# A gated mix of a state-space layer and a two-layer network: the state product of the last two chunks as seven block products, with its skip term scaled by ScalarE and added by DMA

## The chip, the cores and the metric

The kernel runs on one core of one Trainium2 chip. The metric is device microseconds of one execution. A core has TensorE (PE, with its weight loads PEld), VectorE (DVE), ScalarE (ACT), GpSimd (POOL) and SyncE (SP), which run side by side, each through its own list of instructions in order, and wait for each other by semaphores. SP, ACT and POOL can start transfers (DMA).

## The reference, cut to what matters

The input x has 2048 rows of 640 columns. A gate per row mixes a diagonal complex state-space layer with a dense network.

```python
g = sigmoid((x * gate_w).sum(-1, keepdims=True))
# state layer
Bu = einsum("bld,pd->blp", x, B_bar)              # 640 complex states
for t in range(L):
    h = Lam_bar * h + Bu[:, t, :]                 # one step per row
y = 2.0 * einsum("blp,dp->bld", hseq, C).real + x * Dskip
# dense layer
b = gelu(x @ w1 + b1) @ w2 + b2                   # 640 -> 1728 -> 640
return g * y + (1 - g) * b
```

So the state product is hs (2048 x 1280: real and imaginary parts) times CT (1280 x 640), and x * Dskip is its skip term.

## The kernel before, in words

The 2048 rows go in four chunks of 512, each of four row tiles of 128. For each chunk there are four stages of TensorE work:

- `ssm(c)`: x times B, 50 matmuls of 512 columns. ScalarE copies each result out of PSUM (L610). VectorE then runs, for each of five state tiles, a rotation (f1 to f3: wa, wb, v at L533), two scans along time (L555) and a rotation back (f6 to f8: wa, wb, hs at L533).
- `ff1(c)`: x times w1 in 13 tiles and a narrow last one, each through a gelu on ScalarE (L308).
- `fin_b(c)`: the dense second product, already as seven block products. The hidden matrix of a chunk is cut into two row halves and two inner halves (a, b; s1, d), w2 into two inner and two column halves. Sums and differences of these blocks (N2, N3, TA, TB, TC) are made by ScalarE negations (`minus`, L655) followed by accumulating transfers (`plus`, L650) from the POOL queue. PSUM results are copied between banks by ScalarE (`fork`, L714), and what leaves is scaled by 1 - g into a tile `gb` (`out_of`, L722). Product Q is scaled into `gq` (`part_7`, L735) and added by one transfer per row tile to both halves of `gb`.
- `fin_a(c)`: the state product, plain: for each row tile and column half ten matmuls of 320 columns (L775). Before them ScalarE has copied the skip term x * Dskip, which VectorE made (`skip`, L635), into the PSUM bank (`seed`, L641), and the matmuls add to it. VectorE scales the sum by g, adds `gb` (L780) and SP stores the row tile (L790).

The order is written out by hand at the end of the program. VectorE's work is put into a list by `later` with a due time and a cost; `let_out` and `dve_now` let it out in that order as a hand-kept clock of TensorE moves on. So every engine has a fixed order, and `at` hooks place small steps between the products. From chunk 3 on it reads:

```python
    ssm(3)
    gel_tile(3)
    ff1(3)
    gates(3)
    skips(2)
    fin_b(2, seeds(2, lambda: minus_c(3)))
    minus_d(3)
    fin_a(2)
    skips(3)
    fin_b(3, seeds(3))
    let_out(1e9)
    fin_a(3)
```

PSUM has eight banks, and a bank is handed on when its last reader is done. Rows of x for the skip term are loaded into five rotating tiles `xn`.

Of the kernel before, what the change touches and what calls it, by code (L numbers as in the profile page):

```python
# [16 lines left out]
P = 128  # L17
# [25 lines left out]
def kernel(  # L43
# [41 lines left out]
    xT = [xA, xB, xB, xA]  # L85
    w1a = [const.tile([P, cut1], BF16, name=f"w1a_{kd}") for kd in range(KD)]
    w1b = [const.tile([P, cut2 - cut1], BF16, name=f"w1b_{kd}") for kd in range(KD)]
    w1c_lo = const.tile([P, 3, n1c], BF16, name="w1c_lo")
    w1c_hi = const.tile([P, 2, n1c], BF16, name="w1c_hi")
# [39 lines left out]
    def load_w1a(queue, kd):  # L129
        queue.dma_start(out=w1a[kd][:], in_=B_w1[kd * P:(kd + 1) * P, 0:cut1])  # L130

# [394 lines left out]
    def scan_ops(c, ks, bu, ready):  # L526
# [5 lines left out]
        def tt(o, a, b, op):  # L532
            nc.vector.tensor_tensor(out=o, in0=a, in1=b, op=op)  # L533
# [115 lines left out]
    def plus(dst, src):  # L649
        nc.gpsimd.dma_start(out=dst, in_=src, accum_op=ALU.add)  # L650
# [39 lines left out]

    def fin_b(c, at={}):
        (a, b), (s1, d) = blocks(c)
# [38 lines left out]
        def part_7():  # L731
            for j in range(H):
# [26 lines left out]
        settle()  # L759

    def fin_a(c, at={}):
        let_out(0, c)
        for a in range(TPC):
            ti = c * TPC + a
            lo = a * P
            ot = fwork.tile([P, D], BF16, name="ot", bufs=3)
            if a < TPC - 2:
# [3 lines left out]
            for i, (d0, d1) in enumerate(cuts(ti)):  # L771
                p = seeded[ti][i]
                for j in range(2 * KS):
                    CT = CT_re if j < KS else CT_im
                    nc.tensor.matmul(p[:, 0:d1 - d0], lhsT=hs[c][:, j, lo:lo + P], rhs=CT[:, j % KS, d0:d1],  # L775
                                     start=False, stop=(j == 2 * KS - 1), skip_group_check=True)
                    pe(d1 - d0)
# [86 lines left out]
```

## Time and profile before

| | |
|---|---|
| median of 3 runs | 211.99 us (211.9 to 212.34) |
| the profiled execution | 212.2 us, span of its instructions 210.4 us |
| granted TensorE clock | 1.00 throughout |
| VectorE, L555 scans that carry a state, 30 | 37.2 us, 1.271 each |
| VectorE, L780 outputs, 33 | 17.5 us, 0.531 each |
| ScalarE, L308 gelu, 52 | 32.9 us, 0.694 each |
| state product of chunk 0, 80 matmuls | 10.87 us |
| dense product of a chunk, 98 matmuls | some 13.3 us |

The page gives each engine's busy time and its share of the span; groups of equal instructions with count, mean duration and the idle time just before them; DMA queues with packets, bytes and the share of 16 engines' time; and the chain of work that ended last, followed back from the last instruction. The busy time of a pipelined engine overlaps at the edges, so two neighbours of 0.54 us can follow each other every 0.46 us.

### The profile page before, as it was taken

The numbers are of one execution on the slowest core, as the hardware profiler recorded it, in microseconds if no ns is written. First come the engines' busy times: TensorE is split into PE (matmuls) and PEld (weight loads), VectorE is DVE, ScalarE is ACT, GpSimd is POOL, SyncE is SP. The second block draws the span as 40 slices with busy tenths as digits, with TensorE's granted clock in tenths as the row PEclk, the third lists the DMA queues.
The fourth block names the chain that finished last, engine by engine and source line by source line (L and its number), as shares of the span: only waits on it lengthen the run. The fifth ranks groups of instructions, "written<-read, shape, count | busy, mean of one in ns | idle before, by whom it ended". The sixth has DMA issues, their size and how long they took to land.

```text
span 210.4 us, 3617 instructions
## 1 busy us (share of the span) xinstructions
PE 204.3 (97%) x1326; PEld 122.0 (58%) x1326; DVE 180.0 (86%) x295; ACT 142.7 (68%) x290; POOL 48.3 (23%) x79
## 2 busy tenths in 40 slices
PE   8999999989999998999999999999999999999994
PEld 5745444444477543576457777544447777767773
DVE  2579999999997899596999999999999999998132
ACT  3499979996768799990674896267586594047600
POOL 8345059314310500031001043200000145010400
PEclk9999999999999999999999999999999999999999
DMA  7999999999997250249842379910001629943721
GB/s 181 243 189 203 199 247 283 205 231 173 158 190 184 38 90 0 62 86 236 189 101 44 78 119 205 234 49 0 0 0 27 125 64 178 215 131 79 112 78 62
DMA packets 42582, 27.82 MB, mean 132 GB/s; under 512 B 26594, under 2 KB 40388, under 8 KB 42564
## 3 DMA queue, kind: packets, MB, share of 16 engines
q1 hardware_dynamic: 36628, 16.21, 32.4%
q0 software_dynamic: 5360, 10.89, 30.2%
q10 hardware_dynamic: 576, 0.49, 0.7%
q8 instruction: 10, 0.16, 0.3%
q14 instruction: 8, 0.07, 0.1%
HBM read 7.79 MB, written 2.62 MB: 49 GB/s over the span
## 4 chain that ended last, share of the span: by engine, by line
PE 45%; DVE 33%; ACT 12%; issue 5%; DMA 3%; SPq 1%; DVEq 0%
PE bank L607 15%; DVE g L555 11%; PE bank L702 10%; PE bank L775 10%; PE bank L299 8%; DVE wa L533 6%; DVE wb L533 6%; ACT gel L308 5%; DVE hs L533 3%; DVE v L533 3%; DMA xn<-in_A_x_dram 3%; DVE ot L780 3%; PE bank L323 1%; DVE xn L635 1%; ACT TB L655 1%
## 5 line engine op out<-in xcount | busy, mean ns | idle before, releaser
L775 PEld LDWEIGHTS <-hs 128*128 128x128 bf16 x330 | 31.6, 98 | 11.9
L555 DVE TENSOR_TENSOR_SCAN g<-r_c,carry,v 128x512 bf16<-128x512 f32 x30 | 37.2, 1271 | 0.8
L610 ACT ACTIVATE bu<-bank 128x512 bf16<-128x512 f32 x40 | 23.1, 594 | 19.0 <-PE bank L607 18.9
L308 ACT ACTIVATE gel<-bank,colB 128x512 bf16<-128x512 f32 (+1 forms) x52 | 32.9, 694 | 3.0 <-PE bank L299 2.8
L702 PEld LDWEIGHTS <-gel 128*128 128x128 bf16 x280 | 27.2, 98 | 11.0
L780 DVE SCALAR_TENSOR_TENSOR ot<-bank,gcol,gb 128x320 bf16<-128x320 f32 (+2 forms) x33 | 17.5, 531 | 11.8 <-PE bank L775 5.1
L775 PE MATMUL bank<-CT_im,hs 128*128 128x320 bf16 (+2 forms) x165 | 27.1, 295 | 0.0
L775 PE MATMUL bank<-CT_re,hs 128*128 128x320 bf16 (+2 forms) x165 | 27.1, 295 | 0.0
L702 PE MATMUL bank<-w_sb,gel 128*128 128x320 bf16 x168 | 24.1, 299 | 0.0
L299 PEld LDWEIGHTS <-w1a 128*128 128x128 bf16 x162 | 14.4, 101 | 11.9
L722 ACT ACTIVATE gb<-bank,gcol 128x320 f32<-128x320 f32 x32 | 16.1, 525 | 6.0 <-PE bank L702 6.0
L714 ACT ACTIVATE bank<-bank 128x320 f32<-128x320 f32 x16 | 6.8, 424 | 16.5 <-PE bank L702 16.5
L650 POOL DMA_DIRECT2D gel<-N x4 | 3.4, 856 | 60.8 <-PE bank L702 51.2
L607 PEld LDWEIGHTS <-BT_im 128*128 128x128 bf16 x100 | 9.8, 98 | 11.8
L607 PEld LDWEIGHTS <-BT_re 128*128 128x128 bf16 x100 | 9.6, 98 | 11.0
L650 POOL DMA_DIRECT2D gb<-gq x8 | 10.4, 1624 | 22.6 <-ACT gb L722 22.6
L533 DVE TENSOR_TENSOR v<-wa,wb 128x1024 bf16<-128x1024 bf16 (+1 forms) x25 | 14.2, 584 | 0.6
L299 PE MATMUL bank<-xA,w1a 128*128 128x128 bf16 (+2 forms) x102 | 14.6, 302 | 0.0
L533 DVE TENSOR_TENSOR wa<-TCOS,bu 128x1024 bf16<-128x1024 bf16 x20 | 13.7, 687 | 0.6
L533 DVE TENSOR_TENSOR wa<-TCOS,g 128x1024 bf16<-128x1024 bf16 x20 | 13.8, 688 | 0.4
L641 ACT ACTIVATE bank<-xn 128x320 f32<-128x320 bf16 (+2 forms) x33 | 12.7, 427 | 1.7 <-DVE xn L635 1.5
L533 DVE TENSOR_TENSOR wb<-TSIN,g 128x1024 bf16<-128x1024 bf16 x20 | 13.7, 683 | 0.0
(146 smaller groups left out, 354.7 us busy)
## 6 DMA issues: line engine op xcount, KB each, us to landing
gb<-gq POOLq DMA_DIRECT2D x8, 320.0 KB, 5.4
out_dram<-ot SPq DMA_DIRECT2D x15, 160.0 KB, 3.8
w_sb<-in_B_w_dram SPq DMA_DIRECT2D x4, 480.0 KB, 6.5
xn<-in_A_x_dram SPq DMA_DIRECT2D x12, 160.0 KB, 3.9
gel<-N POOLq DMA_DIRECT2D x4, 448.0 KB, 4.5
N<-gel POOLq DMA_DIRECT2D x3, 448.0 KB, 4.5
gel<-gel POOLq DMA_DIRECT2D x3, 448.0 KB, 6.4
N<-N POOLq DMA_DIRECT2D x3, 448.0 KB, 7.8
```

The costliest lines, as they stand in the source:

```text
L299: nc.tensor.matmul(p[:, t0:t1], lhsT=w, rhs=xT[c][:, kd, t0:t1], start=(kd == 0) if first is None else first, stop=(kd == last), skip_grou ...
L308: nc.scalar.activation(out=dst, in_=src, func=ACT.Gelu_apprx_tanh, bias=b1_c[p0:p1, kf:kf + 1])
L533: nc.vector.tensor_tensor(out=o, in0=a, in1=b, op=op)
L555: nc.vector.tensor_tensor_scan(s["g"][:, ri, :], r_c[:, ks:ks + 1].to_broadcast([P, CH]), s["v"][:, ri, :], init, ALU.mult, ALU.add)
L607: nc.tensor.matmul(p[:], lhsT=BT[ks >= KSA][:, kd, (ks % KSA if ks < KSA else ks - KSA) * P:][:, 0:P], rhs=xT[c][:, kd, :], start=(kd == 0 ...
L610: nc.scalar.activation(out=bu[:, ri, :], in_=p[:], func=ACT.Identity)
L641: nc.scalar.activation(out=p[:, 0:d1 - d0], in_=xn[ti][:, d0:d1], func=ACT.Identity)
L650: nc.gpsimd.dma_start(out=dst, in_=src, accum_op=ALU.add)
L702: nc.tensor.matmul(p[:, 0:HD], lhsT=lhs[:, s, j * P:(j + 1) * P], rhs=rhs[:, s, :], start=fresh and s == 0, stop=s == KH - 1, skip_group_c ...
L722: nc.scalar.activation(out=gbs[ti][:, h * HD:(h + 1) * HD], in_=quad[j][name][:, 0:HD], func=ACT.Identity, scale=gcol[:, 1, ti:ti + 1])
L775: nc.tensor.matmul(p[:, 0:d1 - d0], lhsT=hs[c][:, j, lo:lo + P], rhs=CT[:, j % KS, d0:d1], start=False, stop=(j == 2 * KS - 1), skip_group ...
L780: nc.vector.scalar_tensor_tensor(out=ot[:, d0:d1], in0=p[:, 0:d1 - d0], scalar=gcol[:, 0, ti:ti + 1], in1=gbs[ti][:, d0:d1], op0=ALU.mult, ...
```

## The change

For chunks 2 and 3, `fin_a` is replaced by `fin_s`, which makes the state product as seven block products of 256 x 640 by 640 x 320 instead of eight. hs is laid out by row half first, so that its four blocks a, b, g21, d lie in one piece each. CT's four blocks are turned once, during ff1(3), into the needed sums: two ScalarE negations (`c_minus`) and four accumulating transfers (`c_sums`), with one plain copy of a block ahead of them. The sums of hs (M2, M3, M4, and g21 + d in place) are made for chunk 2 by two negations, four accumulating transfers and one copy (`h_hooks`, in hooks of fin_b(2)); for chunk 3 by four VectorE operations (`h_sums`). They lie in tiles that are no longer needed.

The skip term no longer goes through PSUM: ScalarE scales x * Dskip by g into `GS` tiles (`gated`), and transfers add these to `gb` (`skip_in`, and for the lower row tiles together with `gq`). For these two chunks all four skip products of a chunk (`skips`) come ahead of fin_b. `xn` has four rotating tiles instead of five; each next load now follows the scaling. The output tile `ot` has four buffers instead of three.

In the matmuls of `fin_s`, X starts as a times C11 and grows by three products; Y takes X's first state plus b times C21; `less` subtracts product Q (kept in `gq`) from X into Z and later into Q's bank; `out_of` is what L780 did.

```diff
-    xnp = ctx.enter_context(tc.tile_pool(name="xnp", bufs=5))
+    xnp = ctx.enter_context(tc.tile_pool(name="xnp", bufs=4))
...
+            dst = hs[c][:].rearrange("p i r k t -> p r i k t")[:, :, :, ks, :]
             if signed:
-                return tt(hs[c][:].rearrange("p (r k) t -> p r k t", r=2)[:, :, ks, :], s["no"][:], s["ns"][:, ::-1, :], ALU.subtract)
+                return tt(dst, to(s["no"][:]), to(s["ns"][:, ::-1, :]), ALU.subtract)
...
-        hs[c] = hsp.tile([P, 2 * KS, CH], BF16, name="hs")
+        hs[c] = hsp.tile([P, 2, 2, KS, HT], BF16, name="hs")
...
-        if ti + 5 < NT:
-            load_xn(ti + 5)
+        if ti + TPC < NT:
+            load_xn(ti + TPC)
...
+    def twice(dst, src):
+        plus(dst.rearrange("p (h d) -> p h d", h=2), src[:].rearrange("p (o d) -> p o d", o=1).to_broadcast([P, 2, HD]))
...
         part_7()
+        for j in range(H if gs else 0):
+            twice(gs[H + j], gq[j])
+        hook(5)
         both("X", s1, TA)
...
         for j in range(H):
-            plus(gbs[c * TPC + H + j][:].rearrange("p (h d) -> p h d", h=2),
-                 gq[j][:].rearrange("p (o d) -> p o d", o=1).to_broadcast([P, 2, HD]))
+            if gs:
+                plus(gbs[c * TPC + H + j][:], gs[H + j])
+            else:
+                twice(gbs[c * TPC + H + j][:], gq[j])
...
+    def c_minus(h):
+        minus((UA, UB)[h], (C11, C22)[h], 1.6)
+
+    def c_sums():
+        for dst, src in ((UA, C12), (C12, UB), (UB, UA), (UC, UB)):
+            plus(dst, src)
...
+    def h_sums(c):
+        (a, b), (g21, d) = h_blocks(c)
+        for out, x, y, op in ((M3, a, g21, ALU.subtract), (g21, g21, d, ALU.add), (M2, a, g21, ALU.subtract), (M4, b, M2, ALU.add)):
+            dve_now(ck.dve, 0.85, lambda: nc.vector.tensor_tensor(out=flat(out), in0=flat(x), in1=flat(y), op=op))
+
+    def gated(c, a):
+        ti = c * TPC + a
+        nc.scalar.activation(out=GS[a], in_=xn[ti][:], func=ACT.Identity, scale=gcol[:, 0, ti:ti + 1])
+        act(0.82)
+        if ti + TPC < NT:
+            load_xn(ti + TPC)
+
+    def skip_in(c):
+        for j in range(H):
+            plus(gbs[c * TPC + j][:], GS[j])
+
+    def h_hooks(c):
+        (a, b), (g21, d) = h_blocks(c)
+        def first():
+            minus(M3, g21, 1.3)
+            plus(flat(M3), flat(a))
+        def second():
+            minus(M2, d, 1.3)
+            plus(flat(g21), flat(d))
+            nc.sync.dma_start(out=flat(M4), in_=flat(b))
+        return first, second, lambda: plus(flat(M2), flat(M3)), lambda: plus(flat(M4), flat(M2))
+
+    def fin_bs(c, h=[lambda: None] * 4):
+        fin_b(c, {0: h[0], 1: lambda: (h[1](), gated(c, H), gated(c, H + 1)), 5: h[2],
+                  2: lambda: gated(c, 0), 3: lambda: gated(c, 1), 4: lambda: (skip_in(c), h[3]())}, GS)
+
+    def fin_s(c, at={}):
...
+        for j in range(H):
+            product(X, j, a, C11, True)
+            product(Q, j, M3, C12, True)
+            Y[j] = bank()
+            nc.scalar.activation(out=Y[j][:, 0:HD], in_=X[j][:, 0:HD], func=ACT.Identity)
...
+            nc.scalar.activation(out=gq[j][:], in_=Q[j][:, 0:HD], func=ACT.Identity)
+            act(0.53)
+        hook(0)
+        for j in range(H):
+            product(X, j, M2, UB)
+            less(Z, j)
+        for j in range(H):
+            product(Y, j, b, C21)
+        hook(1)
+        for j in range(H):
+            product(X, j, s1, UA)
+            product(Z, j, d, UC)
+            less(Q, j)
+            out_of(Q, j, 1, 1)
+        for j in range(H):
+            out_of(Y, j, 0, 0)
...
+        for j in range(H):
+            out_of(Z, j, 1, 0)
+            store(j, 1)
...
+            product(X, j, M4, C22, False, cols)
+            for d0, d1 in cols:
+                out_of(X, j, 0, 1, d0, d1)
...
-    ff1(3)
+    nc.sync.dma_start(out=UC, in_=C21)
+    ff1(3, 0, {1: lambda: c_minus(0), 4: lambda: (c_minus(1), c_sums())})
     gates(3)
     skips(2)
-    fin_b(2, seeds(2, lambda: minus_c(3)))
-    minus_d(3)
-    fin_a(2)
+    skips(2, H)
+    let_out(0, 2)
+    fin_bs(2, h_hooks(2))
+    fin_s(2, {0: lambda: minus_c(3), 1: lambda: minus_d(3)})
     skips(3)
-    fin_b(3, seeds(3))
+    skips(3, H)
+    fin_bs(3)
     let_out(1e9)
-    fin_a(3)
+    h_sums(3)
+    fin_s(3)
```

In the prediction, the five matmuls of one block product and one row tile are called a product; a chunk's `fin_s` has fourteen of them, two for each of the seven.

More of the change, by code (lines that the diff above doesn't have):

```diff
@@ L85 @@
     xT = [xA, xB, xB, xA]
-    w1a = [const.tile([P, cut1], BF16, name=f"w1a_{kd}") for kd in range(KD)]
+    w1a_sb = const.tile([P, KD, cut1], BF16, name="w1a_sb")
+    w1a = [w1a_sb[:, kd, :] for kd in range(KD)]
     w1b = [const.tile([P, cut2 - cut1], BF16, name=f"w1b_{kd}") for kd in range(KD)]
-    w1c_lo = const.tile([P, 3, n1c], BF16, name="w1c_lo")
+    w1c_lo = const.tile([P, 3, n1c + 1], BF16, name="w1c_lo")
     w1c_hi = const.tile([P, 2, n1c], BF16, name="w1c_hi")
@@ L129, in load_w1a @@
     def load_w1a(queue, kd):
-        queue.dma_start(out=w1a[kd][:], in_=B_w1[kd * P:(kd + 1) * P, 0:cut1])
+        queue.dma_start(out=w1a[kd], in_=B_w1[kd * P:(kd + 1) * P, 0:cut1])
     def rows(queue, dst, v):
@@ L166 @@
     HC = CH // 8
-    tfi = work.tile([P, HC], I32, name="e")
+    tfi = work.tile([P, HC], I32, name="e", bufs=1)
     nc.gpsimd.iota(tfi[:], pattern=[[1, HC]], base=0, channel_multiplier=0)
@@ L213, in load_skip @@
             load_x0(nc.sync, a, KA * P, D)
-        load_xn(TPC)
     ctx.enter_context(tc.manual_schedule(engines={E.PE, E.DVE, E.Activation, E.SP, E.Pool}))
@@ L581, in f8 @@
         def f8():
+            to = lambda t: t.rearrange("p r (i t) -> p r i t", i=2)
+            dst = hs[c][:].rearrange("p i r k t -> p r i k t")[:, :, :, ks, :]
             if signed:
-                return tt(hs[c][:].rearrange("p (r k) t -> p r k t", r=2)[:, :, ks, :], s["no"][:], s["ns"][:, ::-1, :], ALU.subtract)
-            tt(hs[c][:, ks, :], s["no"][:, 0, :], s["ns"][:, 1, :], ALU.subtract)
-            tt(hs[c][:, KS + ks, :], s["ns"][:, 0, :], s["no"][:, 1, :], ALU.add)
+                return tt(dst, to(s["no"][:]), to(s["ns"][:, ::-1, :]), ALU.subtract)
+            for r, x, y, op in ((0, s["no"][:, 0:1, :], s["ns"][:, 1:2, :], ALU.subtract), (1, s["ns"][:, 0:1, :], s["no"][:, 1:2, :], ALU.add)):
+                tt(dst[:, r], to(x)[:, 0], to(y)[:, 0], op)
         later(ready, 0.68, f1)
@@ L689, in first_sums, with fin_b @@
         tt(N2[:], a, g21, ALU.subtract)
-    def fin_b(c, at={}):
+    def twice(dst, src):
+        plus(dst.rearrange("p (h d) -> p h d", h=2), src[:].rearrange("p (o d) -> p o d", o=1).to_broadcast([P, 2, HD]))
+    def fin_b(c, at={}, gs=None):
         (a, b), (s1, d) = blocks(c)
@@ L758, in fin_b @@
         out_of("X", 0, 1)
-        settle()
+        hook(4)
     def fin_a(c, at={}):
@@ L764, in fin_a @@
             ti = c * TPC + a
-            lo = a * P
-            ot = fwork.tile([P, D], BF16, name="ot", bufs=3)
+            ot = fwork.tile([P, D], BF16, name="ot", bufs=4)
             if a < TPC - 2:
@@ L774, in fin_a @@
                     CT = CT_re if j < KS else CT_im
-                    nc.tensor.matmul(p[:, 0:d1 - d0], lhsT=hs[c][:, j, lo:lo + P], rhs=CT[:, j % KS, d0:d1],
+                    nc.tensor.matmul(p[:, 0:d1 - d0], lhsT=hs[c][:, a // H, j // KS, j % KS, (a % H) * P:][:, 0:P], rhs=CT[:, j % KS, d0:d1],
                                      start=False, stop=(j == 2 * KS - 1), skip_group_check=True)
@@ L790, in fin_a @@
                 nc.sync.dma_start(out=out2d[ti * P:(ti + 1) * P, :], in_=ot[:])
-    def skips(c):
-        skip(c * TPC)
-        skip(c * TPC + 1)
+    narrow = lambda t, n: t.rearrange("p k t -> p (k t)")[:, 0:n]
+    UA, UB, UC = (narrow(t[:], KS * HD).rearrange("p (k d) -> p k d", k=KS) for t in (BT_re[1], BT_im[1], xB))
+    M2, M3 = (t[:].rearrange("p k t -> p (k t)").rearrange("p (k t) -> p k t", k=KS) for t in (BT_im[0], BT_re[0]))
+    M4 = narrow(xA[:], KS * HT).rearrange("p (k t) -> p k t", k=KS)
@@ new lines, with h_blocks @@
+    GS = [narrow(w1a_sb[:], 4 * D)[:, j * 2 * D:(j + 1) * 2 * D].bitcast(F32) for j in range(2)]
+    GS += [xA[:].rearrange("p k t -> p (k t)")[:, KS * HT:].bitcast(F32), narrow(w1c_lo[:], 2 * D).bitcast(F32)]
+    C11, C12, C21, C22 = (t[:, :, h * HD:(h + 1) * HD] for t in (CT_re, CT_im) for h in range(2))
+    def c_minus(h):
[3 more added lines that the diff above has]
+            plus(dst, src)
+    def h_blocks(c):
+        return [[hs[c][:, i, r] for r in range(2)] for i in range(2)]
@@ new lines, in fin_s, with product, less, out_of @@
+    def fin_s(c, at={}):
+        let_out(0, c)
+        (a, b), (s1, d) = h_blocks(c)
+        X, Y, Z, Q, gq = ([None] * H for _ in range(5))
+        ots = {}
+        def product(t, j, lhs, rhs, fresh=False, cols=((0, HD),)):
+            if fresh:
+                t[j] = bank()
+            for d0, d1 in cols:
+                for ks in range(KS):
+                    nc.tensor.matmul(t[j][:, d0:d1], lhsT=lhs[:, ks, j * P:(j + 1) * P], rhs=rhs[:, ks, d0:d1],
+                                     start=fresh and ks == 0, stop=ks == KS - 1, skip_group_check=True)
+                    pe(d1 - d0)
+            let_out(ck.pe)
+        def less(out, j):
+            t = out[j] = out[j] or bank()
+            dve_now(ck.pe + 0.2, 0.52, lambda: nc.vector.tensor_tensor(out=t[:, 0:HD], in0=X[j][:, 0:HD], in1=gq[j][:], op=ALU.subtract))
+        def out_of(t, j, half, h, d0=0, d1=HD, wait=0.2):
+            ti = c * TPC + half * H + j
+            if ti not in ots:
+                ots[ti] = fwork.tile([P, D], BF16, name="ot", bufs=4)
+            o = h * HD
+            dve_now(ck.pe + wait, 0.54, lambda: nc.vector.scalar_tensor_tensor(
+                out=ots[ti][:, o + d0:o + d1], in0=t[j][:, d0:d1], scalar=gcol[:, 0, ti:ti + 1],
+                in1=gbs[ti][:, o + d0:o + d1], op0=ALU.mult, op1=ALU.add))
+        def store(j, half, d0=0, d1=D, queue=None):
+            ti = c * TPC + half * H + j
+            (queue or nc.sync).dma_start(out=out2d[ti * P:(ti + 1) * P, d0:d1], in_=ots[ti][:, d0:d1])
+        def hook(i):
+            if i in at:
+                at[i]()
+            settle()
+        for j in range(H):
[3 more added lines that the diff above has]
+            nc.scalar.activation(out=Y[j][:, 0:HD], in_=X[j][:, 0:HD], func=ACT.Identity)
+            act(0.45)
+            gq[j] = fwork.tile([P, HD], F32, name="gq", bufs=2)
+            nc.scalar.activation(out=gq[j][:], in_=Q[j][:, 0:HD], func=ACT.Identity)
+            act(0.53)
+        hook(0)
+        for j in range(H):
[11 more added lines that the diff above has]
+            out_of(Y, j, 0, 0)
+        tail = c == NCH - 1
+        for j in range(H):
+            out_of(Z, j, 1, 0)
+            store(j, 1)
+            last = tail and j == H - 1
+            cols = ((0, 192), (192, HD)) if last else ((0, HD),)
+            product(X, j, M4, C22, False, cols)
+            for d0, d1 in cols:
+                out_of(X, j, 0, 1, d0, d1)
+            if not last:
+                store(j, 0)
+            else:
+                store(j, 0, 0, HD + 192)
+                store(j, 0, HD + 192, D, nc.scalar)
@@ L796, in seeds, with skips @@
+    def skips(c, a=0):
+        skip(c * TPC + a)
+        skip(c * TPC + a + 1)
     def seeds(c, more=lambda: None):
```

## The prediction

> **What bounds the kernel now.** I read the busy shares and the DMA queues on the page, then the chain of waits, then the timeline and stretches of three microseconds around the last two chunks.
>
> ```profile
> PE 204.3 (97%) x1326; PEld 122.0 (58%) x1326; DVE 180.0 (86%) x295; ACT 142.7 (68%) x290; POOL 48.3 (23%) x79
> ...
> q1 hardware_dynamic: 36628, 16.21, 32.4%
> q0 software_dynamic: 5360, 10.89, 30.2%
> ...
> PE 45%; DVE 33%; ACT 12%; issue 5%; DMA 3%; SPq 1%; DVEq 0%
> ```
>
> TensorE is busy nearly always, but a third of the chain is VectorE. In order of time:
>
> ```profile
> 177.05 0.70 DVE v L533
> 177.78 0.06 DVE g L555
> ...
> 186.78 0.04 issue
> 186.83 9.78 PE bank L702 x70
> 196.60 10.90 PE bank L775 x90
> 207.53 0.35 DVE ot L780
> ```
>
> From 119 to 186 us the chain is mostly VectorE (the scans of chunks 2 and 3 and what feeds them); from 186.8 TensorE carries it to the end. So matmuls saved in chunk 3 could count, while chunk 2's state product runs beside a full VectorE:
>
> ```profile
> 177.78 1.28 DVE L555 TENSOR_TENSOR_SCAN g<-r_c,carry,v 128x512 bf16<-128x512 f32 x1
> 178.98 0.98 DVE L780 SCALAR_TENSOR_TENSOR ot<-bank,gcol,gb 128x320 bf16<-128x320 f32 x2
> 179.88 1.27 DVE L555 TENSOR_TENSOR_SCAN g<-r_c,carry,v 128x512 bf16<-128x512 f32 x1
> 182.75 3.97 PE L702 MATMUL bank<-w_sb,gel 128*128 128x320 bf16 x28
> ```
>
> The DMA engines, by stretch (busy time and count of PE, PEld, DVE, ACT, POOL; clock; DMA share; GB/s):
>
> ```profile
> 173.00:176.00 3.00, 3.00 (x24) 2.16 (x23) 2.93 (x6) 2.77 (x5) 2.60 (x3) 1.00 1.04 189
> 176.00:179.00 3.00, 3.00 (x24) 2.16 (x23) 2.93 (x5) 0.00 (x0) 0.88 (x1) 1.00 1.05 164
> 179.00:182.00 3.00, 3.00 (x24) 2.16 (x23) 3.00 (x6) 0.00 (x0) 0.00 (x0) 1.00 1.15 220
> 182.00:185.00 3.00, 3.00 (x24) 2.16 (x23) 2.97 (x7) 0.57 (x2) 0.00 (x0) 1.00 1.03 243
> ```
>
> They are already full from 173 to 185 us. So two resources have no slack where work is added.
>
> **What is removed.** TensorE: 80 matmuls per state chunk become 70. Eighty took 10.9 us (87.5 to 98.3), 0.136 each: 1.36 us per chunk, 2.7 in all. ScalarE: the eight seed copies of a chunk (L641, 0.43 each, 3.4) become four scalings of 640 columns (0.83 each as L507, 3.3): even. VectorE's four skip products (L635) and eight outputs (L780) per chunk stay.
>
> **What is added on ScalarE.** Negations at L655 took 1.687 us for 1792 columns and 2.06 for 2240, so 0.19 + columns/1200: 1.52 for each c_minus (1600), 1.26 for M3 and M2 of chunk 2. The two c_minus lie in ff1(3), where ScalarE idles 0.39 us in each of most tiles; by my count the lag peaks at 1.8 us (two banks) and is gone by tile 12: nothing. Without that idle time they would cost up to 3. M3's negation stands directly ahead of the fork (L714), which began at 159.89: the fork is 1.2 us later, and TensorE waits for it 1.1 us at the second dense product. The state product of chunk 2 then starts near 173.0 instead of 171.8. The negations for chunk 3's N3 and N2 (1.69 each) move from fin_b(2) behind chunk 2's four copies out of PSUM, where ScalarE was idle until 183.9: nothing, since their transfers wait behind M4's anyway. Without that idle time they would hold up the fork of chunk 3 by 3.4.
>
> **What is added on VectorE.** Four subtractions (less) per chunk, four sums (h_sums) in chunk 3. No row subtracts from PSUM into PSUM; L780 (320 columns out of PSUM) took 0.54, 0.46 back to back, the floor; one with both PSUM sides could take the 0.54. I take 0.47 (same 320 fp32 elements). h_sums: 1792 columns took 1.09 (L685), 1024 took 0.69, so 0.82 for 1280, 3.3 in all. They stand in fin_b(3), after the last hs; in before VectorE had 4.3 us idle at 193.7. That cover holds only while fin_b(3) is no earlier. The four-dimensional hs write (L533, 0.69) I leave at 0.69; 0 to 0.1 more each would be up to 1 us on ten of them.
>
> Order decides. The first less of chunk 2 stands behind the whole scan pair: VectorE reaches 177.8 as before (the same four skips, only earlier), both scans take 2.46, so less starts at 180.24. Then: two less 0.95, wa, wb, hs 2.0, less and output 0.94, wa 0.65, less 0.47: 185.3. The last state product writes the bank that this less reads, so it ends at 186.1 to 186.3, while the plain state product of before ended at 182.75. Behind it queues fin_b(3) and all that follows. Each output now also waits for its tile's skip add (L650 into gb), and behind such a wait on VectorE stand the next less, the last scans and chunk 3's sums; by the sums below the adds land at 181.7 to 187, each before its output, so I count nothing, and up to 3 us where POOL's line is slower. So even with free DMA, 3.5 us are lost there.
>
> In chunk 3 the outputs bunch. After the first s1 product ends (6.12 us into nine products of 0.68), VectorE has twelve operations of 0.47, of which the last wait little: last output at 6.12 + 5.4 = 11.5 us, against 11.45 now (196.44 to 207.88). The 1.36 us saved are gone. Four stores, 0.62 MB, then leave within 1.5 us instead of spread over 11; at the 204 GB/s found below they take 3.0 us from the first output on top of the fixed part, so I put 3.2 after the last output against 2.5 now. Sum with free DMA: 186.3 + 13.7 (fin_b(3) as now, 182.75 to 196.44) + 11.5 + 3.2 = 214.7.
>
> **What is added on DMA.** The POOL queue is one line: 30.2% of 210.4 us for 10.89 MB is 171 GB/s while it runs alone, and a transfer adds about 1.8 us:
>
> ```profile
> gel<-N POOLq DMA_DIRECT2D x4, 448.0 KB, 4.5
> ...
> N<-N POOLq DMA_DIRECT2D x3, 448.0 KB, 7.8
> ...
> TB<-TA POOLq DMA_DIRECT2D x1, 320.0 KB, 3.8
> ```
>
> 0.459 MB / 171 = 2.7, plus 1.8 is 4.5; 0.328 MB gives 3.7 against 3.8. The 7.8 is what a queued one pays. Both queues together moved 204 GB/s in the four full stretches above.
>
> c_sums are three links of some 4.1 us that wait for each other (issued 148.2, 152.3, 156.4), in an idle stretch; the fourth, UC, goes out at 160.5, and everything else on POOL stands behind it. Served from 161.4, in this order: UC 0.41 MB, M3 0.33, gel 0.46, g21 0.33, two gq 0.66, M2 0.33, four skip adds 1.31, M4 0.33: 4.15 MB. Beside them on SP: M4's copy, four xn loads, chunk 3's turned tile: 1.15. To the end of M2: 3.66 MB / 204 = 17.9 us: landed 0.8 later, at 180.1 (a share of the 1.8); the fifth product wants it at 173.0 + 4 x 0.68 = 175.7. To the end of M4: 5.3 / 204 = 26.0 us: landed at 188.2; wanted at 184 to 185. Were the SP traffic free, M2 lands at 177 and M4 at 186.6; were both rates simply added, at 181.7 and 191.2. I take the middle, which is a rate measured with both queues running. Then fin_s(2) ends at 188.2 + 1.4 = 189.6.
>
> Chunk 3's own three sums (N3, g21, N2: 1.38 MB) and 0.66 MB of stores now queue behind M4: 2.03 / 204 = 10 us, N2 at 198.2; fin_b(3) wants it at 189.6 + 5.7 = 195.3: 2.9 us more. fin_b(3) ends at 189.6 + 13.4 + 2.9 = 205.9, then 11.5 and 3.2: 220.6; with SP free 217.0. I take 219.5 between them, since shares above 1 in those stretches say the queues overlap somewhat. The profiled run took 212.2 with span 210.4; the median 211.99 is 1.6 over that span. Forecast 219.5 + 1.6 = 221.1.
>
> The Trainium skill, page "DMA: Bandwidth & Descriptors", section "Measured (HBM→SBUF, 128 partitions, SWDGE, issued from GpSimd)", gives 341 GB/s for 1 MB loads from that queue. By that rate the 5.3 MB would take 15.5 us, an estimate from the page, M4 would be there at 178, and the free-DMA sum would hold; the rows of this case show accumulating transfers at half of it, so the sum goes by the rows. The skill's main page, "Trainium Kernel Development and Optimization", section "Key Constraints", says that transfers issued from SP, ACT and POOL interleave on the same 16 engines; it speaks against spreading this work over queues, and no run here shows it apart.
>
> **The rivals.**
> Forecast (0.53): POOL's line is late for M2, M4 and N2. For it: share 1.0 already, 4.5 to 9 us landings. Range 217 to 224.
> VectorE alone (0.25): the sums land in time and only the order of less costs. For it: shares above 1. Against: 5.3 MB in 24 us. 214.7 + 1.6 = 216.3.
> Worse (0.15): c_sums, whose rows in CT are 640 B pieces, take 5 to 6 us a link; UC and all behind it come 3 to 5 us later: 224.5 to 227.
> Faster (0.05): the saved matmuls show. With M3's 1.1 us kept, chunk 2 would end at 173.0 + 9.5 = 182.5, 0.25 earlier, and chunk 3 give its 1.36: 211.99 - 1.6 = 210.4. It decides if the less ahead of the last product ends by 181.8. For it: a later row can't be seen to wait before the edit. Against: every VectorE operation counted above has its own row, and they reach 185.3.
> Doesn't do what it says (0): the built order holds 70 matmuls per chunk. No change by balance: 0.02.
>
> **How the numbers follow.** Slower by over 0.2% (0.4 us, about what a measurement of this kernel can tell): 0.53 + 0.25 + 0.15 = 0.93; within 0.02; faster 0.05. The range takes in the VectorE case and most of the worse one, 215.5 to 226; beyond it lie faster, same and the far end of worse.
>
> **What would show it.** Right: fin_s(2) has TensorE idle some 4 us before its fifth product, waiting for the transfer into BT_im, and again before the last two, for xA; fin_b(3) starts near 189.6; DMA share near 1 from 162 to 198; VectorE's first less near 181. Wrong: M2 landed by 176 (then VectorE alone), TensorE without a gap between 160 and 205 (then faster), or a first wait already in fin_b(2) for gel (then worse).

## The result, and the profile after

The changed kernel took 227.6 us (median of four runs, 227.02 to 229.02) against 212.1 for the kernel before: a ratio of 1.074 [1.069, 1.079]. The forecast was 221.1 with a range to 226.0. The profiled execution has a span of 225.2 us. Its page, with the busy shares, the granted clock in forty slices, the POOL queue and the chain by engine:

```profile
PE 204.1 (91%) x1301; PEld 120.5 (54%) x1301; DVE 187.3 (83%) x307; ACT 150.6 (67%) x293; POOL 63.5 (28%) x95
...
PEclk9999999999999999999999999999999699699997
...
q0 software_dynamic: 8688, 16.46, 42.8%
...
PE 47%; DMA 24%; ACT 12%; issue 7%; DVE 4%; POOL 3%; SPq 1%; DVEq 0%; POOLq 0%; ACTq 0%
```

TensorE works as long as before (204.1 us against 204.3) although it has 25 recorded matmuls fewer: in two slices of its work the clock was below full (the third low digit is the last slice, where TensorE is done). In the chain DMA has taken VectorE's place, 24% where it had 3%. The stretch from 168 to 198 us, first of the kernel before, then of the changed one (busy time and count of PE, PEld, DVE, ACT, POOL; clock; DMA share; GB/s):

```profile
168.00:198.00 30.00, 29.89 (x220) 21.27 (x219) 25.25 (x39) 16.50 (x35) 8.36 (x8) 1.00 0.63 126
```

```profile
168.00:198.00 30.00, 19.58 (x121) 12.58 (x120) 19.19 (x31) 9.97 (x16) 10.92 (x12) 0.89 1.08 215
```

Where TensorE had no gap, it now lacks ten of thirty microseconds, and the DMA engines are full. The four waits of TensorE in that stretch and just before it, from its timeline (start, length, then in brackets the idle time ahead and what ended it):

```profile
160.62 2.06 PE L707 MATMUL bank<-w_sb,gel 128*128 128x320 bf16 x14 [1.05 <-ACT bank L719]
...
175.01 3.68 PE L707 MATMUL bank<-w_sb,gel 128*128 128x320 bf16 x14 [4.73 <-DMA gel<-N]
...
183.14 1.53 PE L865 MATMUL bank<-BT_im,BT_im 128*128 128x320 bf16 x10 [1.73 <-DMA BT_im<-BT_re]
...
192.71 2.83 PE L865 MATMUL bank<-CT_im,xA 128*128 128x320 bf16 x10 [3.97 <-DVE ot L879]
```

The first is M3's negation ahead of the fork. The second is the last dense product of chunk 2, which waits for gel's add; the two after it wait for M2 and M4 (BT_im and xA). The last wait is put down to VectorE, which had been done; the weight load beside it, PEld, waited 4.3 us for xA, so it is the transfer. Of equal work, 14 matmuls, the one behind 4.73 us of idle time took 3.68 us instead of 2.06; the ten behind 3.97 took 2.83 instead of 1.53. The ten behind 1.73 were not slower.

Why gel's add came late stands in POOL's timeline. Names leave buffer numbers out: of the four tiles for sums of CT, UA lies in BT_re, UB in BT_im, UC in xB, and C12 is a half of CT_re; M3 lies in another BT_re, M2 in another BT_im and M4 in xA.

```profile
147.48 1.51 POOL L652 DMA_DIRECT2D BT_re<-CT_re  x1 [15.80 <-ACT BT_re L657]
153.16 1.50 POOL L652 DMA_DIRECT2D CT_re<-BT_im  x1 [4.17 <-DMA BT_re<-CT_re]
158.90 0.88 POOL L652 DMA_DIRECT2D BT_im<-BT_re  x1 [4.23 <-PE bank L707]
165.06 0.86 POOL L652 DMA_DIRECT2D xB<-BT_im  x1 [5.28 <-DMA BT_im<-BT_re]
...
166.15 1.54 POOL L652 DMA_DIRECT2D gel<-N  x1
```

The four C sums leave 5.68, 5.74 and 6.16 us after one another, since each overwrites what the one before read or reads what it wrote. The fourth (UC) stands at the head of the queue until 165.06, and what is behind it, ready or not, stands too. At the end of the program VectorE waits again, for the skip sums of the lower row tiles of chunk 3:

```profile
218.24 0.55 DVE L879 SCALAR_TENSOR_TENSOR ot<-bank,gcol,gb 128x320 bf16<-128x320 f32 x1 [0.79 <-DMA gb<-w1a_sb]
219.88 2.51 DVE L879 SCALAR_TENSOR_TENSOR ot<-bank,gcol,gb 128x320 bf16<-128x320 f32 x6 [1.09 <-DMA gb<-w1a_sb]
```

### The profile page after: what moved, and what is told of

Same layout as the page of the kernel before. It is cut to its first block, busy times and chain, and to the rows that moved or that the text cites. A ratio compares the mean times of both kernels' runs of the same rounds, so it can differ in the third digit from the quotient of the medians.

```text
span 225.2 us, 3624 instructions
## 1 busy us (share of the span) xinstructions
PE 204.1 (91%) x1301; PEld 120.5 (54%) x1301; DVE 187.3 (83%) x307; ACT 150.6 (67%) x293; POOL 63.5 (28%) x95
## 4 chain that ended last, share of the span: by engine, by line
PE 47%; DMA 24%; ACT 12%; issue 7%; DVE 4%; POOL 3%; SPq 1%; DVEq 0%; POOLq 0%; ACTq 0%
PE bank L609 19%; PE bank L785 10%; DMA w1c_lo<-gq 9%; PE bank L299 8%; PE bank L707 7%; ACT gel L308 5%; DMA N<-gel 5%; DMA gb<-w1a_sb 3%; DMA N<-N 2%; DMA CT_re<-BT_im 2%; DMA BT_re<-CT_re 2%; PE bank L258 1%; POOL gb L652 1%; DVE g L555 1%; PE bank L323 1%
## 5 line engine op out<-in xcount | busy, mean ns | idle before, releaser
L707 PE MATMUL bank<-w_sb,gel 128*128 128x320 bf16 x168 | 25.9, 312 | 5.8 <-DMA gel<-N 4.7
L299 PEld LDWEIGHTS <-w1a_sb 128*128 128x128 bf16 x162 | 14.0, 98 | 11.9
L785 PEld LDWEIGHTS <-hs 128*128 128x128 bf16 x160 | 15.6, 98 | 6.0
L872 DVE TENSOR_TENSOR bank<-bank,gq 128x320 f32<-128x320 f32 x8 | 4.0, 498 | 14.4 <-PE bank L865 14.4
L533 DVE TENSOR_TENSOR wa<-TCOS,bu 128x1024 bf16<-128x1024 bf16 x20 | 13.7, 686 | 0.5
L299 PE MATMUL bank<-xA,w1a_sb 128*128 128x128 bf16 (+2 forms) x102 | 14.0, 293 | 0.0
L533 DVE TENSOR_TENSOR wb<-TSIN,bu 128x1024 bf16<-128x1024 bf16 x20 | 13.7, 684 | 0.0
L533 DVE TENSOR_TENSOR wb<-TSIN,g 128x1024 bf16<-128x1024 bf16 x20 | 13.7, 684 | 0.0
L785 PE MATMUL bank<-CT_re,hs 128*128 128x320 bf16 x80 | 13.5, 299 | 0.0
L785 PE MATMUL bank<-CT_im,hs 128*128 128x320 bf16 x80 | 13.5, 299 | 0.0
L299 PE MATMUL bank<-xB,w1a_sb 128*128 128x512 bf16 x60 | 13.3, 379 | 0.0
L707 PEld LDWEIGHTS <-N 128*128 128x128 bf16 x112 | 10.9, 98 | 4.3
```

The costliest lines, as they stand in the source:

```text
L299: nc.tensor.matmul(p[:, t0:t1], lhsT=w, rhs=xT[c][:, kd, t0:t1], start=(kd == 0) if first is None else first, stop=(kd == last), skip_grou ...
L707: nc.tensor.matmul(p[:, 0:HD], lhsT=lhs[:, s, j * P:(j + 1) * P], rhs=rhs[:, s, :], start=fresh and s == 0, stop=s == KH - 1, skip_group_c ...
L785: nc.tensor.matmul(p[:, 0:d1 - d0], lhsT=hs[c][:, a // H, j // KS, j % KS, (a % H) * P:][:, 0:P], rhs=CT[:, j % KS, d0:d1], start=False, s ...
L872: dve_now(ck.pe + 0.2, 0.52, lambda: nc.vector.tensor_tensor(out=t[:, 0:HD], in0=X[j][:, 0:HD], in1=gq[j][:], op=ALU.subtract))
```

## The experiments

The theory after the result: POOL's line of transfers costs the time, because the C sums hold it up and its bytes are too many; against it stood VectorE's order (the subtractions behind the scans), ScalarE's negation ahead of the fork, and the lowered clock. Ratios are to the kernel before, which took 212.3 to 212.5 us beside these runs; they are those on record and can differ by some 0.2% from the quotient of the medians.

### e1, none of the added transfers

```diff
-        for dst, src in ((UA, C12), (C12, UB), (UB, UA), (UC, UB)):
-            plus(dst, src)
...
-            plus(flat(M3), flat(a))
...
-        for j in range(H):
-            plus(gbs[c * TPC + j][:], GS[j])
```

(and so for the other new calls of `plus`; Q's addition into `gb`, which the kernel before has as well, is left out with them for these two chunks)

> Leaves out every transfer that the change added on the POOL queue (the sums of CT and of hs, the two additions of gq, the skip adds into gb), so the output lacks these terms; all matmuls, VectorE and ScalarE work stay. Theory 1 (POOL's line of accumulating transfers costs the time): 211.5 to 213.5 us, no TensorE wait above 2 us from 157 us on, clock 1.00 throughout, the first less starting at 177 and fin_s(2) ending near 183. Theory 2 (VectorE's order costs it): most of the loss stays, 216 us or more, with TensorE waiting for a less 3 us or more. Theory 3 (with transfers free, the 2.7 us of matmuls show): 210 or less.

Measured: 213.6 us, 1.0035 [1.0009, 1.0062], 0.1 above the first theory's range. Of the 15.5 us lost, 14 go with these transfers. POOL's queue moves 9.58 MB here and 10.89 in the kernel before, so the run is a little freer than "without the added ones". What is left is small but no gain: seven products instead of eight bring nothing even where the transfers are free.

### e2 and e3, one half of the transfers each

In e2 `c_sums` returns at once; in e3 the eight sums of GS into gb are left out.

> Leaves out the four sums of CT (output differs), all else as in the change. Theory 1: POOL's line is free at 160 us, so the transfer into gel (4.7 us wait and 1.6 us at a lower clock) lands in time; M2 and M4 land 5 to 8 us earlier: 217 to 221 us. If those four are only in an idle stretch and block nothing: 226 or more.

> Leaves out the eight transfers that add the GS tiles into gb (output lacks skip term and Q in two chunks). Theory 1: the first wait in fin_b(2) stays (4 to 5 us), M4 lands 5 us or more earlier and the last outputs no longer wait: 218 to 222 us. Theory 2: 226 or more, since VectorE's count is the same.

Measured: e2 221.63 us, 1.041 [1.037, 1.046]; e3 222.73 us, 1.044 [1.036, 1.053]; both a little above their ranges. In e2 nothing waits for gel any more, but M2's product waits 2.67 us and M4's 3.48. In e3 the wait for gel stays (5.08 us) and those for M2 and M4 are nearly gone (0.62, none). So the C sums make the wait in the dense product, and the bytes of the skip sums the wait for M4. M2's sum is issued ahead of the skip sums and lands 10.8 us later in both kernels (172.34 to 183.14, and 176.59 to 187.41 in e3); its shorter wait in e3 only says that TensorE came later, behind more time at a lowered clock. Neither half gives back more than six of the fourteen microseconds.

### e4, UC behind gel's add

```diff
-        for dst, src in ((UA, C12), (C12, UB), (UB, UA), (UC, UB)):
+        for dst, src in ((UA, C12), (C12, UB), (UB, UA)):
...
             minus(M2, d, 1.3)
+            plus(UC, UB)
             plus(flat(g21), flat(d))
```

> The same work; only the fourth sum of CT is issued after the addition into gel instead of before it. If the line's order (head of line) makes the first wait: no wait for gel in fin_b(2), clock 1.00 there, 6 us less at the start of fin_s(2), of which M2 and M4 take some back since the bytes are the same: 221 to 225 us. If the bytes alone make it: 227 to 228, the wait only moved.

Measured: 224.59 us, 1.055 [1.051, 1.059]. POOL's and TensorE's timelines:

```profile
164.21 0.86 POOL L652 DMA_DIRECT2D gel<-N  x1 [1.58 <-PE bank L707]
164.82 1.12 POOL L652 DMA_DIRECT2D xB<-BT_im  x1
...
181.27 1.67 POOL L652 DMA_DIRECT2D xA<-BT_im  x1
```

```profile
171.35 2.06 PE L707 MATMUL bank<-w_sb,gel 128*128 128x320 bf16 x14
...
181.03 2.52 PE L866 MATMUL bank<-BT_im,BT_im 128*128 128x320 bf16 x10 [4.90 <-ACT N L657]
...
198.56 2.08 PE L707 MATMUL bank<-TB,N 128*128 128x320 bf16 x14 [1.62 <-DMA N<-N]
```

gel's add now leaves as soon as TensorE has read b (POOL waited for PE, not for a link), and the dense product runs without a wait and at full clock. Three microseconds are gained. The wait for M2 grows from 1.73 to 4.90 and N2's from nothing to 1.62, while M4's falls from 3.97 to 1.38. (The wait of 4.90 is put down to ScalarE; the weight load beside it waited 5.23 us for the transfer into BT_im.) Much of a wait that is removed at one sum shows up at the next.

### e5, the changed buffers alone

```diff
-    xnp = ctx.enter_context(tc.tile_pool(name="xnp", bufs=5))
+    xnp = ctx.enter_context(tc.tile_pool(name="xnp", bufs=4))
...
-            ot = fwork.tile([P, D], BF16, name="ot", bufs=3)
+            ot = fwork.tile([P, D], BF16, name="ot", bufs=4)
```

> The kernel before with only the change's buffers: four output tiles instead of three, four tiles of xn instead of five, and so no wait of VectorE for an output tile (2.17 us in the trace before, at 100.33). Theory: VectorE's lead is not on the path, since TensorE sets the end and VectorE had slack in front of it, so 211.6 to 212.6. Rival: the 2.2 us by which VectorE ran ahead in the changed kernel are worth as much by themselves, so some 210.

Measured: 211.95 us, 0.9963 [0.9937, 0.9990]. In the kernel before VectorE had this wait, which the prediction did not see:

```profile
100.33 0.55 DVE L780 SCALAR_TENSOR_TENSOR ot<-bank,gcol,gb 128x320 bf16<-128x320 f32 x1 [2.17 <-DMA out_dram<-ot]
```

Without it the chain by engine reads `PE 78%; ACT 12%; DVE 3%`, where VectorE had 33%. Most of the 2.2 us is slack, as the theory held; the 0.37% of the ratio are 0.8 us (0.2 to 1.3), the medians lie 0.4 apart.

### e6, TensorE kept busy through the wait

```diff
         hook(3)
+        for _ in range(32 if at.get(0) else 0):
+            nc.tensor.matmul(quad[0]["Y"][:, 0:HD], lhsT=a[:, 0, 0:P], rhs=W(0, 0)[:, 0, :], start=True, stop=True, skip_group_check=True)
         both("X", b, W(1, 1))
```

> The changed kernel with 32 products of 128x320 put into TensorE's idle time ahead of the last dense product of chunk 2 (into a bank that has been read), some 4.7 us of work. They compute nothing that is used. If the idle time causes the lowered clock, the 14 matmuls of that product take about 2.1 us again instead of 3.68 and the granted clock stays near 1. Theory: the transfers behind them set the pace up to the fourth sum of the state parts, so the saved 1.6 us turn into a longer wait ahead of the next product and the time stays at 226.5 to 228.5. Rival: the low clock costs by itself, so 225.0 to 226.0.

Measured: 229.57 us, 1.082 [1.074, 1.089], above both expectations. The 32 products ran in chunk 3 as well, which was not meant and cost 4.35 us there (206.99 to 211.34), so the total decides nothing and the stages must. (Taking the 4.35 off gives 225.2, in the rival's range; but the delay also let the skip sums of chunk 3 land, and the two waits of 1.9 us at the end are absent in this run.)

```profile
170.91 4.51 PE L769 MATMUL bank<-w_sb,gel 128*128 128x320 bf16 x32
175.82 2.08 PE L707 MATMUL bank<-w_sb,gel 128*128 128x320 bf16 x14 [0.40 <-DMA gel<-N]
...
184.67 2.85 PE L867 MATMUL bank<-BT_im,BT_im 128*128 128x320 bf16 x10 [4.06 <-DMA BT_im<-BT_re]
...
201.28 2.08 PE L707 MATMUL bank<-TB,N 128*128 128x320 bf16 x14 [1.25 <-DMA N<-N]
```

Without the idle time the 14 matmuls took 2.08 us again. So idle time lowers the clock, and it is no cost of the transfers themselves. M2's wait grew from 1.73 to 4.06, and the slow matmuls moved behind it. Counted from the start of fin_b(2), chunk 3's dense product began 2.0 us sooner than in the changed kernel (35.9 against 37.9 us), but the product that needs N2 only 0.6 sooner (43.0 against 43.6).

### e7 and e8, the sums in the order of need

e7 issues the first C sum beside its negation. e8 does that too, puts M3's negation behind the fork, M2's sum ahead of the two `twice`, M4's ahead of the skip sums, the lower tiles' skip sums in halves, and the loads of `xn` later. Of e8's edits:

```diff
-        hook(0)
         both("X", a, W(0, 0), True)
         fork("X", "Y")
+        hook(0)
...
-        for j in range(H if gs else 0):
-            twice(gs[H + j], gq[j])
         hook(5)
+        for j in range(H if gs else 0):
+            twice(gs[H + j], gq[j])
...
         out_of("Z", 1, 0)
+        hook(6)
...
-    2: lambda: gated(c, 0), 3: lambda: gated(c, 1), 4: lambda: (skip_in(c), h[3]())}, GS)
+    2: lambda: (gated(c, 0), gated(c, 1)), 6: h[3], 3: lambda: skip_in(c, 0), 4: lambda: skip_in(c, 1)}, GS)
```

> The changed kernel with the first of the four C sums issued right after its own negation, three hooks earlier in the third chunk's first dense layer; nothing else is changed. Theory (the chain of the C sums is too long and stands ahead of gel's add on the queue): the last C sum is issued some 5.7 us earlier (at about 159.4 instead of 165.06 on the trace's scale), gel's add right after its release (about 163), so the 4.73 us wait and the slow clock behind it go, about 2 us of it come back as a wait for the second state sum: 221.5 to 224.5. Rival (the bytes alone set the pace, the chain is only where it shows): 226.5 to 228.

> The changed kernel with its transfers in the order in which they are needed: first C sum early, the negation of the state part behind the copies of the first dense product, the second state sum ahead of the two copies of the last part, the fourth state sum ahead of the skip sums, the skip sums of the lower tiles in halves, the loads of the next chunk's xn later. Theory: order was worth most of the loss, bytes the rest: up to the fourth state sum some 4.4 MB must pass between 161 and 184, which at 204 GB/s ends about 2 us late; 216 to 220. Rival (the bytes set all of it): over 222. In neither case below 212.5.

Measured: e7 228.55 us, 1.075 [1.067, 1.083]; e8 228.03 us, 1.071 [1.063, 1.078]. Both of my theories fell, but e7 tests neither of its two, as it was no change at all: in the changed kernel the first C sum had already left 0.3 us after its negation ended (147.19 and 147.48), since POOL had nothing ahead of it. What sets the chain's start is the negation on ScalarE, not the place of the call. e8 kept the wait for gel (5.13 us), but did what it was to do in the state product, whose waits fell to 0.42 us, so that chunk 3's dense product began at 188.17 instead of 195.35. Nearly all of it was lost again:

```profile
194.07 2.08 PE L707 MATMUL bank<-w_sb,N 128*128 128x320 bf16 x14 [1.73 <-DMA N<-gel]
200.54 3.91 PE L707 MATMUL bank<-TB,N 128*128 128x320 bf16 x14 [4.40 <-DMA N<-N]
```

The product that needs N2 began at 200.54, in the changed kernel at 201.08. So e8's rival stood: what counts is when the line has brought everything up to N2 of chunk 3. The order only chooses at which sum TensorE waits.

### e9 and e10, the line started sooner, and the line shortened

e9 is e8 with UC behind chunk 2's gel sum and the first two of its four state sums (M3, and g21 + d); e10 is e9 without the skip sums.

> The ordered kernel, and the last of the four C sums issued behind chunk 2's gel and state sums instead of ahead of them. Theory (POOL's queue is one line that runs full up to N2's sum of chunk 3; whatever is put first, the last one pays): what stands behind the C sums is issued some 3 us earlier, N2's sum at about 191.5 instead of 194.64, and the end comes 2.5 to 3 us earlier than in the ordered kernel: 224.5 to 226. Rival (the wait for gel is the loss by itself): its 5.13 us and the slow clock behind it, 1.9 us, both go: 220.5 to 222.

> The kernel of e9 without its eight skip sums into gb (two chunks, so the output lacks the skip term). 1.31 MB less in chunk 2. Theory: at 204 GB/s that is 6.4 us ahead of N2's sum, which is then no longer waited for, and the state sums are there in time: 215.5 to 219. Rival (the order of VectorE and the clock cost the rest): not under 221.

Measured: e9 224.15 us, 1.054 [1.051, 1.058]; e10 216.69 us, 1.021 [1.018, 1.023]. e10 is inside the theory's range, e9 0.35 us below it and far above the rival's. The line's end and the program's end, from the timelines (e2 to e4 had different starts, so times are also counted from the start of fin_b(2)):

| | fin_b(2) starts | N2's sum issued | its product starts | from there to the end | from fin_b(2) to the product |
|---|---|---|---|---|---|
| changed | 157.50 | 195.37 | 201.08 | 24.1 | 43.6 |
| e8 | 157.16 | 194.64 | 200.54 | 24.5 | 43.4 |
| e9 | 157.22 | 191.54 | 197.67 | 23.8 | 40.5 |
| e4 | 158.73 | 192.88 | 198.56 | 24.2 | 39.8 |
| e3 | 161.43 | 195.45 | 200.27 | 22.1 | 38.8 |
| e2 | 158.25 | 190.09 | 195.80 | 23.0 | 37.6 |
| e10 | 157.44 | 187.32 | 192.86 | 22.0 | 35.4 |

The way from that product to the end is 22 to 24.5 us in all seven, the longer ones where VectorE waits at the end for the skip sums of chunk 3 (1.9 us in the changed kernel and e4, 0.8 in e2, none in e8 and e9) or where TensorE multiplies at a lowered clock behind its wait for N2 (2.4 us more in e8, 1.7 in e9). The way to it spans eight. In the changed kernel and in e2 TensorE does not wait at N2 itself: it has already waited as long for M4, on the same line.

In e10 it is no longer the bytes ahead of it on the line that hold N2 up. POOL stood idle for 5.98 us ahead of N3's sum, which waited for its negation on ScalarE; and ScalarE was late because it waited 5.40 and then 1.81 us for the two transfers that read the `gq` tiles (`twice`), since the state product writes these tiles again (ScalarE's copies of Q, at 177.53 and 180.11). TensorE's and POOL's timelines:

```profile
178.35 1.49 PE L865 MATMUL bank<-BT_im,BT_im 128*128 128x320 bf16 x5 [2.73 <-ACT bank L896]
```

```profile
182.43 0.86 POOL L652 DMA_DIRECT2D N<-gel  x1 [5.98 <-ACT N L657]
```

TensorE's wait of 2.73 us comes from the same two tiles, in e9 too. What more `gq` tiles would be worth is not tested.

### e11, the last chunk alone

Chunk 2 stays as before. C12's sum goes into a tile of its own (CN), and chunk 3's state sums are VectorE's, as in the change.

```diff
-    fin_bs(2, h_hooks(2))
-    fin_s(2, {0: lambda: minus_c(3), 1: lambda: minus_d(3)})
+    fin_b(2, seeds(2, lambda: minus_c(3)))
+    minus_d(3)
+    minus(CN, C22, 1.6)
+    plus(CN, C12)
+    fin_a(2)
...
-            product(Q, j, M3, C12, True)
+            product(Q, j, M3, CN, True)
```

> The change made in the last chunk alone, with the changed buffers: chunk 2 as before, with seeds; the four C sums in a tile of their own where C12 must be kept; VectorE makes chunk 3's four state sums, as in the change. No state sums by DMA, no skip sums in chunk 2. Theory: nothing waits in chunk 2, the 1.36 us of matmuls saved in chunk 3 go to the outputs that bunch and to skip sums that land late: 211.0 to 213.5. Rival (saved matmuls show): 209.5 to 210.8, which would beat both kernels.

Measured: 213.47 us, 1.0063 [1.0039, 1.0087]. TensorE has no gap from 159 to 206, and VectorE ends the run: two waits for gb (0.39 and 1.13 us) and then six outputs in a row.

```profile
206.28 0.55 DVE L882 SCALAR_TENSOR_TENSOR ot<-bank,gcol,gb 128x320 bf16<-128x320 f32 x1 [0.39 <-DMA gb<-w1a_sb]
207.96 2.51 DVE L882 SCALAR_TENSOR_TENSOR ot<-bank,gcol,gb 128x320 bf16<-128x320 f32 x6 [1.13 <-DMA gb<-w1a_sb]
```

The profiled execution took 215.16 us, the longest of ten, but the stage shows the loss by itself: from the start of fin_b(2) to the end of the last output it takes 50.8 us, where e5 takes 48.9. This run also holds two links of the C sums in a stretch without other traffic, the first with strided pieces and the second without:

```profile
149.62 1.51 POOL L653 DMA_DIRECT2D BT_re<-CT_re  x1 [15.80 <-ACT BT_re L658]
155.31 0.91 POOL L653 DMA_DIRECT2D BT_im<-BT_re  x1 [4.18 <-PE bank L300]
159.72 0.86 POOL L653 DMA_DIRECT2D xB<-BT_im  x1 [3.51 <-DMA BT_im<-BT_re]
```

0.91 + 3.51 = 4.4 us, where the same bytes read as 640-byte pieces took 1.51 + 4.18 = 5.7.

### e12 and e13, where the saved matmuls go when transfers are free

e12 is e1 with M3's negation behind the fork; e13 also writes the outputs of Y in chunk 3 at once:

```diff
         for j in range(H):
             product(Y, j, b, C21)
+            if tail:
+                out_of(Y, j, 0, 0)
```

> As e1 (none of the added POOL transfers, so the state products of the seven-product form multiply unsummed blocks and the skip term is missing), with the negation of the state part behind the copies of the first dense product. Theory: the 1.05 us wait of TensorE at the second dense product goes, so 212.2 to 213.0 against 213.6 for e1, and with free transfers the change is worth nothing: not below 211.8. Rival: with that wait gone the saved 2.7 us of matmuls show, 210.5 or less.

> As e12 (no added POOL transfers, the negation behind the copies), and in the last chunk the two outputs of the third quarter's product (Y) are written as soon as its matmuls end, in a stretch where VectorE waits 1.47 us, instead of behind the four subtractions. Theory (the saved matmuls are hidden by VectorE's outputs that bunch at the end): two outputs of 0.45 leave the bunch, 0.9 us earlier end: 211.0 to 211.6, where e12 took 212.26. Rival (the bunch is not the end's limit): 212.0 to 212.5.

Measured: e12 212.26 us, 1.0000 [0.9983, 1.0017]; e13 211.39 us, 0.9957 [0.9939, 0.9974]. In e12 the waits of chunk 2's state product, for VectorE's subtractions, take 1.85 us, more than the 1.36 saved there:

```profile
177.45 0.84 PE L859 MATMUL bank<-BT_re,hs 128*128 128x320 bf16 x5 [1.10 <-DVE bank L866]
...
181.77 0.84 PE L859 MATMUL bank<-CT_im,xA 128*128 128x320 bf16 x5 [0.75 <-DVE bank L866]
```

and in chunk 3 VectorE ends e12 with eight outputs, e13 with six:

```profile
204.02 3.43 DVE L873 SCALAR_TENSOR_TENSOR ot<-bank,gcol,gb 128x320 bf16<-128x320 f32 x8
```

```profile
201.18 1.23 DVE L873 SCALAR_TENSOR_TENSOR ot<-bank,gcol,gb 128x320 bf16<-128x320 f32 x2
...
204.43 2.51 DVE L873 SCALAR_TENSOR_TENSOR ot<-bank,gcol,gb 128x320 bf16<-128x320 f32 x6
```

Taking two outputs out of the bunch moved the end by what they take, 0.9 us. So the bunch is the limit there. Even so e13 stands where e5 does (0.9963), which has the same buffers and all eight products.

### e14, the last chunk alone, mended

e11 with CN in five tiles, Y's outputs early, and the first halves of the lower tiles' skip sums ahead of the upper tiles'.

> The change in the last chunk alone, as e11, with the summed C12 kept in the five tiles of the first layer's middle weights, the early Y outputs of e13, and the skip sums of the lower tiles in halves, the first half ahead of the upper tiles' sums. Theory: against e11 the two waits of VectorE for gb (0.39 and 1.13 us) go and 0.9 us of outputs, 213.47 - 2.4 = 211.1: 210.3 to 212.0, at or below both kernels. Rival (POOL's sums of the last chunk remain late by their bytes, 1.31 MB at 171 GB/s from 193 on): 212.5 to 213.5.

Measured: 211.46 us, 0.9966 [0.9944, 0.9989]. Of VectorE's waits for gb 0.17 us remain. It ends below the kernel before, by as much as the changed buffers alone (e5, 0.9963), which it contains. Its last state product with outputs takes 10.9 us (196.64 to 207.49) against 11.4 in e5 (195.78 to 207.22), but about half a microsecond in one stage is not told apart in these totals. A version that beats both kernels exists, then; that the seven products have a part in it is not shown.

## Why the prediction fell short

The direction was right, and so was the main mechanism: POOL's line is late for M2, M4 and N2. Its length was wrong, and its first victim was missed: the forecast had no wait for gel in fin_b(2), where TensorE waited 4.73 us. The step that failed is "c_sums are three links of some 4.1 us that wait for each other ... the fourth, UC, goes out at 160.5". The links took 5.68, 5.74 and 6.16 us, and UC went out at 165.06. The price had come from transfers whose pieces are long, and for those it holds (4.4 in e11). The first two links read or write 640-byte pieces, for which POOL itself took 1.5 us instead of 0.9 and the rest 4.2 instead of 3.5. The third has long pieces and took 6.16 beside chunk 3's turned tile on SP, 4.4 in e11, where it ran before that tile. With UC out of the way of gel's add (e4) the kernel was 3.0 us faster. The rival "Worse" had this very mechanism, with links of 5 to 6 us, and got 0.15; its 224.5 to 227 lies just under the result, and the sign named for it, a first wait already in fin_b(2) for gel, is what the trace shows.

The Trainium skill, page "Perfetto Trace Analysis", section "DMA Instruction — SWDGE (GPSIMD)", says that the profiled time of such an instruction on POOL is the writing of its descriptors and not the moving of the data. This trace agrees: 0.88 and 1.51 us on POOL for equal bytes that took 5.7 to 6.2 us from issue to issue.

From forecast to result, 221.1 to 227.6:

- UC went out 4.6 late. M2 landed at 183.1 instead of 180.1 (3.0) and M4 at 192.7 instead of 188.2 (4.5); M4's product then ran at a lowered clock, 1.3 more. fin_s(2) ended at 195.35, forecast 189.6. N2 landed at 201.0 instead of 198.2 (2.8), and the forecast wait of 2.9 us for it did not come, as TensorE was there no sooner. Together 2.8 at the end of fin_b(3) (208.69 against 205.9).
- Chunk 3's state product and outputs took 13.7 us, forecast 11.5: 2.2, of which 1.9 are the two waits for the lower skip sums at the end. The prediction counted those sums for chunk 2 and put nothing for chunk 3, without a reason.
- The end after the last output took 2.8, forecast 3.2: 0.4 less. The sum by its own terms was 220.6; choosing 219.5 "between them" took away 1.1 that were there. The median lies 2.4 over the span instead of 1.6: 0.8.

2.8 + 2.2 - 0.4 + 1.1 + 0.8 = 6.5. The rate in the sum was near: 204 GB/s were taken, 215 measured in the full stretch.

Other steps. M3's negation cost 1.05 us (1.1 forecast). The subtraction took 0.498 us each (0.47 forecast, between 0.46 and 0.54) and VectorE's state sums 0.83 (0.82). Outputs that bunch: 11.6 us in e12 (11.5 forecast), and e13 shows that they are the limit. The twelve operations of 0.47 behind it would make 5.6 us and not the 5.4 of the sum; in e12 they took 5.3 (202.13 to 207.45). The four stores are 0.66 MB, not 0.62. VectorE's order was put too dear: 214.7 for the span with free transfers against 212.1 in e1. VectorE had lost 2.2 us to the wait for an output tile, and with a fourth one chunk 2's last scans begin at 174.61 instead of 177.78, 1.06 of that by an earlier start of the whole run. In e12 the subtraction ahead of the last product ended at 181.72, just where the rival "Faster" was to decide, and nothing was gained, since the products before it had waited too. The c_minus cost nothing on TensorE, but they set when the chain of links begins.

## What to carry to other kernels

A block scheme that saves an eighth of the matmuls pays with sums. Here the sums and the skip term, now added by DMA, sent 2.7 MB more in thirty microseconds (215 against 126 GB/s) through DMA engines that were already 63% busy. Count the bytes up to the last transfer that TensorE needs, divide by the rate measured with all queues running, and add the length of every chain of dependent transfers ahead of them, with the price of rows that have the same piece size. A dependent link at the head of an in-order queue holds up everything behind it, so independent sums go first; but reordering only moves the wait along while the line's end stays where it is. When the engine that feeds the outputs is the next limit, spread its work into its gaps before saving work elsewhere.

## What the runs showed of the hardware

How long TensorE had been idle does not settle by itself when the granted clock falls. Read in windows of 0.1 us from 155 us on, it fell to half 2.28 us after TensorE had gone idle in e7, 4.62 and 3.23 us after in the changed kernel, and 5.28 us after in e4, where TensorE was already working again. No wait of up to 2.67 us (e2) brought it down; in e9 and e10 one of 2.73 us did, 2.4 us after its start. In all thirteen falls that came while TensorE had work left (changed kernel, e2 to e4, e6 to e10) it stayed at half for 3.4 us (changed kernel, 174.91 to 178.32 and 191.97 to 195.39) or for 6.8 us (e7, 173.74 to 180.57; e6, 183.36 to 190.19). The stretch behind the idle time of e7 shows the clock at half:

```profile
174.00:177.00 3.00, 0.82 (x4) 0.48 (x5) 2.93 (x5) 0.00 (x0) 0.36 (x1) 0.50 1.05 225
177.00:180.00 3.00, 3.00 (x13) 1.74 (x12) 1.24 (x2) 0.53 (x1) 0.00 (x0) 0.50 1.14 242
180.00:183.00 3.00, 3.00 (x21) 1.91 (x19) 0.00 (x0) 1.81 (x4) 0.86 (x1) 0.91 1.17 216
```

The Trainium skill, page "TensorE: Matmul & The Clock Gate", section "Part 1: The HAM clock gate", states half the clock after an idle window of about 3.4 us and full clock after about as long a busy one; the half is what these rows show, and the shorter spells of 3.4 us fit the second figure. The falls 2.3 to 2.4 us into a wait (e7, e9) are earlier than the first figure, and the spells of 6.8 us twice the second; here the measurement decides. What a low clock costs is half of the time that TensorE works under it: behind waits of 4 to 5 us this was 1.3 us (of 2.7, from 192.71 to 195.39 in the changed kernel) to 2.8 us (of 5.5, from 184.67 to 190.19 in e6), where nothing behind waits anyway.
